# A limit of six transfers in flight on SyncE's queue, in a cosine attention with a token-mixing MLP behind it

## The chip, the cores and the metric

The kernel runs on one core of one Trainium2 chip. A core has five engines with their own instruction streams: TensorE (PE in the profile, its weight loads PEld), VectorE (DVE), ScalarE (ACT), GpSimd (POOL) and SyncE (SP), and 16 DMA engines that move data between memory and the on-chip buffers. SP here does nothing but issue transfers. The metric is device microseconds of one execution. Before the change the median of six runs is 131.78 us (129.74 to 132.66).

## The reference

Eight batches, eight heads, 576 positions, 64 features per head, all in float32. The first part is a linear attention whose features are weighted by the cosine and sine of the position, the second a mixing of tokens:

```python
theta = pi/2 * arange(576)/576
q_p = concat(relu(q)*cos(theta), relu(q)*sin(theta))    # per head, 128 features
k_p = concat(relu(k)*cos(theta), relu(k)*sin(theta))
kv  = einsum('bhsf,bhsd->bhfd', k_p, v);  z = sum(k_p, over s)
x   = (q_p @ kv) / (q_p . z + 1e-6)                     # heads joined: (8, 576, 512)
wq, wk = x @ w_q, x @ w_k                               # 512 -> 64
mixed  = (wq @ wk.T / 8) @ x
out    = relu(mixed) @ w_out                            # (8, 576, 512)
```

## The kernel before

The 64 heads are taken two at a time: a tile holds two heads, one on each half of the 128 partitions, with 9 rows of 64 features in each partition, which is 128 x 576 float32 or 288 KB. Two such tiles make one step H (0 to 15), with halves s = 0 and 1. So q, k and v come in as 96 loads of 288 KB each; the weights come in three more, the output leaves in 42 stores of 128 or 256 KB.

For each step the loads `LD` (line 203) fill the float32 tiles `raw` (a ring of `N_RAW` = 4 steps for each of k, q and v; the profile names them kf, qf, vf). `RK` (relu of k) and `MK` (times cosine and sine) make `kp`, `CV` casts v to `vb`, `DQ` makes relu of q twice side by side in `qd`. `QK` on TensorE forms k'v and transposes q; `EK` and `EQ` bring both out of PSUM, `NM` makes numerator and denominator, `RC` and `XN` divide, which gives `xs`. After the four pairs of a batch: `XT`, `WQK`, `TK`, `KX`, `MX`, `WO` are the products of the second part, `EX`, `EW`, `EWK`, `EKX`, `EMX`, `EO` their way out of PSUM, and `ST` (line 422) stores from `osb`, a ring of `N_OSB` = 6.

The order of all this is written out by hand in `ORDER` (line 37): words such as `LD.k.14.0@Y` name an operation, its step and half, and the engine (Y SyncE, A ScalarE, V VectorE, G GpSimd, T TensorE with a PSUM bank). Each engine executes its words strictly in that order. The framework adds the semaphores: an instruction waits for what it reads and for the users of the buffer that it overwrites. The load of k for step 14, for example, overwrites the tile of step 10 and waits for `RK.10.0@A`; everything behind it on SyncE waits with it. The 129 transfers of SyncE are the 96 loads, the three loads of weights (`LW`, lines 213 to 216) and 30 of the stores, in the order of the words; 12 stores are ScalarE's. Completion of transfers is told by eight semaphores that are taken in turn by all transfers in the order of the program; a transfer whose semaphore was used before waits for the landing of that earlier transfer.

Of the kernel before, what the change touches and what calls it, by code (L numbers as in the profile page):

```python
# [24 lines left out]
N_RAW, N_RK, N_KP, N_QD, N_VB, N_QPT, N_KV = 4, 2, 3, 3, 3, 4, 4  # L25
N_XS, N_XT, N_WQK, N_WKJ, N_KX, N_MIX, N_OSB = 3, 2, 2, 2, 2, 2, 6
# [3 lines left out]
SPLIT = (0, 1, 2, 3, 4, 5, 6, 7, 8, 9, 10, 11, 12, 13, 14, 15)  # L30
UNITS = (((0, 1), (2, 3)), ((0,), (1, 2), (3, 4)))
UNITS7 = ((0,), (1, 2), (3,), (4,))
N_FIRST, N_WARM = 9, 14


# [74 lines left out]
def kernel(  # L110
# [14 lines left out]
    DH = moe_w_q.shape[1]  # L125
    P = 128
# [12 lines left out]
    def ring(name, shape, dtype, n):  # L139
        return [consts.tile(shape, dtype, name=f"{name}{i}") for i in range(n)]  # L140

    raw = {t: ring(f"{t}f", [P, 2, HC], FP32, N_RAW) for t in "kqv"}
# [14 lines left out]
    osb = ring("osb", [P, 2, DM], FP32, N_OSB)  # L157
    w_f = consts.tile([P, NDM, 2 * DH], FP32, name="w_f")
    wo_f = consts.tile([P, NDM, DM], FP32, name="wo_f")
# [21 lines left out]
    A, V, G, T, Y = nc.scalar, nc.vector, nc.gpsimd, nc.tensor, nc.sync  # L181
# [18 lines left out]
    def part(H, s):  # L200
        return (s, s + 1) if H in SPLIT else (0, 2)

    def LD(eng, pb, t, H, s):
        lo, hi = part(H, s)
        b, h = divmod(H, 2)
        step = 1 if LD_PAIR else hi - lo
        for i in range(lo, hi, step):
            eng.dma_start(raw[t][H % N_RAW][:, i:i + step, :],  # L208
                          srcs[t][b][:, 2 * h + i:2 * h + i + step, :])

    def LW(eng, pb, w):
        if w == "qk":
            eng.dma_start(w_f[:, :, 0:DH], moe_w_q.rearrange("(c p) j -> p c j", p=P))
            eng.dma_start(w_f[:, :, DH:2 * DH], moe_w_k.rearrange("(c p) j -> p c j", p=P))
        else:
            eng.dma_start(wo_f, moe_w_out.rearrange("(c p) n -> p c n", p=P))

    def CW(eng, pb, w, s=0):
        if w == "qk":
# [172 lines left out]
    def EMX(eng, pb, b, j):  # L392
# [9 lines left out]
        else:  # L402
            eng.tensor_scalar(dst, src, scale_moe, 0.0, op0=ALU.mult, op1=ALU.max)

    units = [(b, u, ts) for b in range(B)
             for u, ts in enumerate(UNITS7 if b == B - 1 else UNITS[b % 2])]
    unit_of = {(b, t): (n, ts) for n, (b, u, ts) in enumerate(units) for t in ts}
# [14 lines left out]
    def ST(eng, pb, b, u, hi):  # L422
        ts = (UNITS7 if b == B - 1 else UNITS[b % 2])[u]
        n, _ = unit_of[b, ts[0]]
        bl, c = divmod(2 * (ts[0] + 4 * (b % 2)) + hi, C9)
        row = ((b // 2) * 2 + bl) * S + c
        dst = dataclasses.replace(
            out, offset=out.offset + row * DM,
            ap=[[C9 * DM, 64], [2 * DM, len(ts)], [1, DM]])
        eng.dma_start(dst, osb[n % N_OSB][64 * hi:64 * hi + 64, 0:len(ts), :])  # L430

    ops = dict(LD=LD, LW=LW, CW=CW, RK=RK, MK=MK, CV=CV, DQ=DQ, QK=QK, EK=EK, EQ=EQ,
               NM=NM, RC=RC, XN=XN, XT=XT, EX=EX, WQK=WQK, EW=EW, DW=DW, TK=TK,
               EWK=EWK, KX=KX, EKX=EKX, MX=MX, EMX=EMX, WO=WO, EO=EO, ST=ST)
    engines = dict(T=T, V=V, A=A, G=G, Y=Y)

# [72 lines left out]
```

## Time and profile before

| | |
|---|---|
| median of six runs | 131.78 us (129.74 to 132.66) |
| profiled execution: time, span | 132.43 us, 130.6 us |
| busy: DVE, PE, ACT, POOL | 105.7, 103.7, 77.4, 70.3 us |
| mean granted TensorE clock | 0.927 |
| transfers: bytes, mean rate | 39.40 MB, 302 GB/s |
| chain that ended last | PE 30%, DVE 29%, DMA 13%, issue 7%, POOL 6%, SP 5% |
| SP's longest wait for an engine | 8.3 us, for ScalarE's relu of k (L193) |

Busy times are those of the engines' data paths; SP has none, since issuing is not counted. "From issue to landing" is the time from the start of the issuing instruction to the last update of the transfer's semaphore. The chain is followed back from the last instruction, at each step to what released it. In views by time the span starts at 0.

### The profile page before, as it was taken

What the parts mean: (1) busy time and instruction counts of PE and PEld (TensorE: products, weight loads), DVE (VectorE), ACT (ScalarE), POOL (GpSimd) and SP (SyncE); (2) the same over time, 40 slices, a digit from 0 to 9 for tenths busy, and PEclk for the clock granted to TensorE, in tenths of its full rate; (3) what the DMA queues carried; (4) which work ended last, traced back from release to release, by engine and by line L of the source; (5) the groups of instructions that cost most, each with busy time, mean ns of one, the idle gap of its engine ahead of it and who ended that gap; (6) DMA issues with size and microseconds to landing.
All of it is one profiled execution on the core that took longest, in us unless ns stands there. A gap on an engine that the chain in (4) does not pass through costs nothing.

```text
span 130.6 us, 5197 instructions
## 1 busy us (share of the span) xinstructions
PE 103.7 (79%) x2198; PEld 68.6 (53%) x2198; DVE 105.7 (81%) x227; ACT 77.4 (59%) x124; POOL 70.3 (54%) x81
## 2 busy tenths in 40 slices
PE   5925694848789979769999939779999979999900
PEld 2315584738577546556667627355676754543400
DVE  3466999897999999999999865899999987774600
ACT  7125443983596688974948828637986644246110
POOL 7009826098969999992095341589949540020000
PEclk9995559595999999999999999999999999999997
DMA  4999999999999999990079999999998897369793
GB/s 149 288 381 406 398 385 376 348 389 385 395 380 390 391 378 393 385 348 29 5 188 374 255 317 385 355 365 328 355 336 331 163 359 219 83 203 282 179 287 100
DMA packets 20711, 39.40 MB, mean 302 GB/s; under 512 B 3280, under 2 KB 3280, under 8 KB 20688
## 3 DMA queue, kind: packets, MB, share of 16 engines
q1 hardware_dynamic: 19152, 36.32, 80.9%
q10 hardware_dynamic: 1536, 2.75, 6.6%
q8 instruction: 17, 0.28, 0.8%
q14 instruction: 6, 0.05, 0.1%
HBM read 29.62 MB, written 9.44 MB: 299 GB/s over the span
## 4 chain that ended last, share of the span: by engine, by line
PE 30%; DVE 29%; DMA 13%; issue 7%; POOL 6%; SPq 5%; ACT 4%; ACTq 2%; POOLq 0%
PE banks L413 13%; DVE kp L232 9%; DMA kf<-in_k_dram 9%; DVE xs L309 8%; DVE qpt L279 6%; DMA qf<-in_q_dram 5%; PE banks L260 4%; PE banks L269 4%; POOL qd L195 3%; SPq L208 3%; DVE rec L305 3%; PE banks L326 2%; SPq L430 2%; PE banks L292 2%; DVE kvs L187 2%
## 5 line engine op out<-in xcount | busy, mean ns | idle before, releaser
L195 POOL TENSOR_SCALAR qd<-qf 128x1152 bf16<-128x1152 f32 x32 | 38.5, 1213 | 13.8 <-DMA qf<-in_q_dram 13.1
L413 PE MATMUL banks<-wo_sb,mix 128*128 128x512 bf16 x144 | 36.0, 380 | 0.0
L232 DVE TENSOR_TENSOR kp<-rk,cossin 128x1152 bf16<-128x1152 bf16 x32 | 28.9, 923 | 1.8 <-POOL rk L195 1.5
L309 DVE TENSOR_TENSOR xs<-banks,rec 128x640 bf16<-128x640 f32 x32 | 25.4, 807 | 0.3
L279 DVE TENSOR_TENSOR qpt<-banks,cst 128x1152 bf16<-128x1152 bf16 x32 | 23.8, 744 | 2.3 <-PE banks L269 2.0
L185 ACT COPY osb<-banks 128x512 f32<-128x512 f32 x31 | 18.0, 589 | 12.8 <-PE banks L413 9.0
L401 ACT ACTIVATE mix<-banks 128x640 bf16<-128x640 f32 (+1 forms) x27 | 17.4, 657 | 10.2 <-PE banks L388 10.0
L260 PE MATMUL banks<-vb,kp 64*128 64x65 bf16 x576 | 16.7, 202 | 6.2 <-ACT vb L185 2.0
L413 PEld LDWEIGHTS <-mix 128*128 128x128 bf16 x144 | 12.1, 98 | 12.5 <-issue 1.6
L260 PEld LDWEIGHTS <-kp 64*128 64x128 bf16 x576 | 13.6, 101 | 9.6 <-issue 3.7
L269 PE MATMUL banks<-ident,qd 64*128 64x64 bf16 x576 | 16.4, 203 | 2.4 <-POOL qd L195 2.4
L292 PE MATMUL banks<-kvs,qpt 128*128 128x65 bf16 x320 | 15.6, 200 | 3.1 <-DVE kvs L187 2.2
L292 PEld LDWEIGHTS <-qpt 128*128 128x128 bf16 x320 | 13.4, 101 | 6.9 <-DVE qpt L279 2.3
L195 POOL TENSOR_SCALAR rk<-kf 128x576 bf16<-128x576 f32 x14 | 12.4, 893 | 6.4 <-DMA kf<-in_k_dram 6.0
L193 ACT ACTIVATE rk<-kf 128x576 bf16<-128x576 f32 x15 | 10.1, 684 | 9.2 <-DMA kf<-in_k_dram 9.2
L189 POOL TENSOR_SCALAR vb<-vf 128x576 bf16<-128x576 f32 x17 | 12.5, 738 | 5.2 <-DMA vf<-in_v_dram 4.1
L269 PEld LDWEIGHTS <-qd 64*128 64x128 bf16 x576 | 13.1, 103 | 2.5 <-POOL qd L195 2.5
L185 ACT COPY xT<-banks 128x1280 bf16<-128x1280 bf16 x10 | 12.3, 1227 | 3.6 <-PE banks L326 3.6
L185 ACT CAST vb<-vf 128x576 bf16<-128x576 f32 x14 | 9.4, 674 | 6.2 <-DMA vf<-in_v_dram 5.9
L326 PE MATMUL banks<-ident,xs 64*128 64x64 bf16 x320 | 7.8, 196 | 5.4 <-DVE xs L309 5.3
L326 PEld LDWEIGHTS <-xs 64*128 64x128 bf16 x320 | 6.4, 99 | 8.5 <-DVE xs L309 5.1
L189 POOL TENSOR_SCALAR wq<-wqk 64x576 bf16<-64x576 bf16 x4 | 2.8, 708 | 14.9 <-DVE wqk L187 7.8
(46 smaller groups left out, 115.0 us busy)
## 6 DMA issues: line engine op xcount, KB each, us to landing
kf<-in_k_dram SPq DMA_DIRECT2D x32, 288.0 KB, 5.9
vf<-in_v_dram SPq DMA_DIRECT2D x32, 288.0 KB, 6.0
qf<-in_q_dram SPq DMA_DIRECT2D x32, 288.0 KB, 5.9
out_dram<-osb SPq DMA_DIRECT2D x21, 256.0 KB, 4.7
out_dram<-osb ACTq DMA_DIRECT2D x9, 256.0 KB, 4.2
out_dram<-osb SPq DMA_DIRECT2D x9, 128.0 KB, 3.5
wo_f<-in_moe_w_out_dram SPq DMA_DIRECT2D x1, 1024.0 KB, 7.9
out_dram<-osb ACTq DMA_DIRECT2D x3, 128.0 KB, 4.1
```

The lines of the kernel that those rows point to most:

```text
L185: A.copy(dst, src)
L189: eng.tensor_scalar(dst, src, 1.0, 1.0, op0=ALU.mult, op1=ALU.mult)
L195: eng.tensor_scalar(dst, src, FMAX, 0.0, op0=ALU.min, op1=ALU.max)
L232: eng.tensor_mul(kp[H % N_KP][:, lo:hi], rk[H % N_RK][:, lo:hi].unsqueeze(3).to_broadcast([P, n, C9, 2, D]), cossin.unsqueeze(1).to_broadc ...
L260: T.matmul(kvp[:, hh, :], kp[H % N_KP][p0:p0 + 64, i, c, :, :], vb[H % N_VB][p0:p0 + 64, i, c, 0:D + 1], start=(c == 0), stop=(c == C9 - 1))
L269: T.transpose(qt[:, hh, c * D:(c + 1) * D], src, ident[p0:p0 + 64, p0:p0 + 64])
L279: eng.tensor_mul(qpt[g % N_QPT][:, :, 1:SLOTS, :], qk_views(at["QK", g])[0].rearrange("f h (c d) -> f h c d", c=C9), cst.unsqueeze(1).to_b ...
L292: T.matmul(nv[:, hh, u, :], qpt[g % N_QPT][:, hh, 2 * u:2 * u + 2, :], kvs[g % N_KV][:, hh, :], start=(u == 0), stop=(u == SC - 1 and not ...
L309: eng.tensor_tensor(xs[b % N_XS][:, :, 2 * pr:2 * pr + 2, :].rearrange("p u h d -> p h u d"), num_view(at["NM", g])[:, :, :, 0:D], rec[g % ...
L326: T.transpose(xv[:, r, i, u, :], xs[b % N_XS][p0:p0 + 64, u, 2 * hp:2 * hp + 2, :], ident[p0:p0 + 64, p0:p0 + 64])
L401: A.activation(dst, src, AF.Relu, scale=scale_moe)
L413: T.matmul(o, mix[b // 2 % N_MIX][:, dmc, base:base + P], wo_sb[:, dmc, :], start=(dmc == 0), stop=(dmc == NDM - 1))
```

## The change

A function `dma` takes the place of the direct calls. It issues as before, keeps a list of the transfers that were issued on SyncE, and from the seventh on makes each of them depend on the one six places ahead in that list, so that it is issued only after that one has landed. Transfers on ScalarE's queue go through the same function and are neither listed nor held.

```diff
+N_FLIGHT = 6
...
+    flight = []
+
+    def dma(eng, dst, src):
+        ins = eng.dma_start(dst, src).ins
+        if eng is Y:
+            if len(flight) >= N_FLIGHT:
+                tc.add_manual_dep(ins, flight[-N_FLIGHT].name, mybir.DependencyInfo(
+                    mybir.DependencyClass.Sync, mybir.DependencyReason.DATA),
+                    reason="limit on transfers in flight")
+            flight.append(ins)
+
     def LD(eng, pb, t, H, s):
...
-            eng.dma_start(raw[t][H % N_RAW][:, i:i + step, :],
+            dma(eng, raw[t][H % N_RAW][:, i:i + step, :],
                           srcs[t][b][:, 2 * h + i:2 * h + i + step, :])
...
-            eng.dma_start(w_f[:, :, 0:DH], moe_w_q.rearrange("(c p) j -> p c j", p=P))
-            eng.dma_start(w_f[:, :, DH:2 * DH], moe_w_k.rearrange("(c p) j -> p c j", p=P))
+            dma(eng, w_f[:, :, 0:DH], moe_w_q.rearrange("(c p) j -> p c j", p=P))
+            dma(eng, w_f[:, :, DH:2 * DH], moe_w_k.rearrange("(c p) j -> p c j", p=P))
         else:
-            eng.dma_start(wo_f, moe_w_out.rearrange("(c p) n -> p c n", p=P))
+            dma(eng, wo_f, moe_w_out.rearrange("(c p) n -> p c n", p=P))
...
-        eng.dma_start(dst, osb[n % N_OSB][64 * hi:64 * hi + 64, 0:len(ts), :])
+        dma(eng, dst, osb[n % N_OSB][64 * hi:64 * hi + 64, 0:len(ts), :])
```

## The prediction

> **What bounds the kernel now.** I read first which stretches are full of transfers, then what SyncE (SP) waits for, then whether a transfer's 6 us is work or queue, and last who uses the data. From the page, the transfer load in 40 slices of 3.27 us and the median time from issue to landing:
>
> ```profile
> DMA  4999999999999999990079999999998897369793
> ...
> kf<-in_k_dram SPq DMA_DIRECT2D x32, 288.0 KB, 5.9
> vf<-in_v_dram SPq DMA_DIRECT2D x32, 288.0 KB, 6.0
> qf<-in_q_dram SPq DMA_DIRECT2D x32, 288.0 KB, 5.9
> ```
>
> The engines that move data are full from 3 to 59 us, empty from 59 to 64, and nearly full again to about 100. SP's own waits up to 54.8 us:
>
> ```profile
> SPq L208 <- DMA qf<-in_q_dram: 7.0, 17, 0.8
> SPq L208 <- DMA vf<-in_v_dram: 6.6, 16, 0.7
> SPq L208 <- DMA kf<-in_k_dram: 6.5, 16, 0.9
> SPq L208 <- DMA wo_f<-in_moe_w_out_dram: 2.3, 1, 2.3
> ```
>
> The reader is to see that SP already waits for landings, about fifty times and 0.4 us each. The trace gives the distance: eight completion semaphores are used in turn, and an issue waits for the landing of the transfer eight earlier (the load issued at 52.44 follows, by 0.06 us, one that landed at 52.38). The kernel before is therefore limited to eight; the change makes that six. SP's timeline shows the pace:
>
> ```profile
> 50.89 0.33 SPq L208 DMA_DIRECT2D qf<-in_q_dram  x1
> 51.66 0.33 SPq L208 DMA_DIRECT2D vf<-in_v_dram  x1
> 52.44 0.33 SPq L208 DMA_DIRECT2D qf<-in_q_dram  x1
> 53.19 0.33 SPq L208 DMA_DIRECT2D kf<-in_k_dram  x1
> ```
>
> An issue takes 0.33 us, one follows the other after 0.75 us, and 288 KB (294,912 bytes) in 0.75 us is 393 GB/s. Eight times 0.75 is 6.0 us, which is the time to landing: most of the 5.9 us may be queue. Two views say that it is. The first load after the pause, issued at 64.44 into empty queues (transfers issued from 64.4 to 64.8 us):
>
> ```profile
> kf<-in_k_dram SPq DMA_DIRECT2D x1, 288.0 KB, 2.8
> ```
>
> The very first load, at 0.74, took 2.7. And the drain: SP issues nothing between 55.2 and 64.4 us, since the load of k for pair 14 waits for ScalarE (8.3 us in SP's waits), so what is in flight falls from eight to none. By stretch (length; busy time of PE, PEld, DVE, ACT, POOL; granted clock; transfer share; GB/s):
>
> ```profile
> 40.00:55.20 15.20, 13.57 (x291) 8.41 (x289) 14.80 (x32) 12.05 (x21) 14.56 (x16) 1.00 1.05 388
> ...
> 55.20:56.20 1.00, 0.91 (x8) 0.73 (x8) 1.00 (x2) 0.62 (x2) 0.92 (x2) 1.00 1.03 385
> 56.20:57.20 1.00, 1.00 (x46) 0.92 (x46) 1.00 (x2) 0.73 (x2) 0.92 (x2) 1.00 1.03 371
> 57.20:58.20 1.00, 0.34 (x19) 0.25 (x12) 0.99 (x3) 0.97 (x3) 1.00 (x2) 1.00 1.01 378
> ```
>
> The rate stays at 371 to 385 GB/s while six, five, four remain, and the last eight landings (55.37 to 60.46) keep a spacing of 0.73 us down to the last one. The transfer engines don't need eight to be full.
>
> Where is data late? Up to 24 us nearly every relu or cast starts 0.02 to 0.2 us after its load's landing; from 24 to 59 DVE is 97% busy (14.80 of 15.20 us above) and loads have 0.1 to 5 us to spare. From 64.4 to 87 loads are just in time again, and the chain that ended last runs through two of them:
>
> ```profile
> 68.43 4.37 DMA kf<-in_k_dram
> ...
> 74.00 7.00 DMA kf<-in_k_dram
> ```
>
> **The change, part by part.** No byte, no transfer and no instruction of another engine is added or moved. Added is one wait on each SP issue but the first six (123 of 129 issues; ScalarE's 12 stores are neither counted nor held).
>
> *Instructions.* Where all transfers are SP's, the new wait covers the old one: the transfer eight earlier was already waited for by the issue two before. So one wait takes the place of one, and its reaction is 0.02 us as now. Where ScalarE's stores lie between (from 73 us), an issue may need a second wait; such separate waits stand in the trace with 0.02 us and some 0.05 us around them. With 12 such stores: 0 to 12 x 0.07 = 0.8 us, and of these only those from 73 to 87, where SP's issues are on the chain, can count (two stores, 0.1 us). I take 0.1 us.
>
> *Start (to 6.6 us).* The seventh issue stands at 3.54 and the transfer six ahead landed at 3.44: no hold. The eighth goes from 4.01 to 4.21, the ninth from 4.75 to 6.57 (landing of the third at 6.55). The ninth landed at 11.09; issued by 6.9 it has 4.2 us left, against 2.8 for a whole lone load. Cost 0; the queue of transfers four to eight covers it.
>
> *Full stretch (6.6 to 55.2 us).* Each issue moves two spacings later: 2 x 0.75 = 1.5 us. Its landing was 5.9 after the issue, so 4.4 remain, and a lone load needs 2.7 to 2.8. The cover is 1.6 us, some two transfers always queued. So landings stay and cost is 0. Behind each held issue on SP stand only later issues, held by the same pace; who waits for them (relu and cast on ACT, POOL, DVE) waits for landings. Without that cover each 0.1 us of spacing would cost 1.7 us on the 17 loads up to 24 us. Behind the 1 MB load of w_out (landed 36.01) two more issues wait (from 32.57 and 33.36 to about 36.03 and 36.8); they landed at 41.22 and 41.96, so about 5 us remain. Cost 0.
>
> *Pause (55.2 to 64.4).* Ended by ScalarE's relu of k at 63.73, which hangs on DVE and PE work. Unchanged.
>
> *Late loads (64.4 to 82).* Here the time goes, so I compared each issue with the landing six before it on SP. Of the issues from 64.44 to 81.69 the tightest stand 0.00 to 0.06 us after it (74.85, 76.43, 77.62, 78.28, 81.69), the rest 0.2 to 7.6 us. On this stretch a six-back wait on SP's list and the present eight-back wait over both queues are nearly the same, since two of ScalarE's stores lie between. Cost 0, with nothing to spare: a hold here would go straight to the end.
>
> *82 to 97.* Holds of 0.1 to 1.5 us; 3.3 to 4.6 us remain to each landing. Here SP issues almost without pause (18 issues from 82.23 to 96.07, 0.77 us each), yet transfers are 101% busy at 350 GB/s, so SP loses run-ahead and not landings. At 96.8 it stands still for ScalarE's copy until 100.39 anyway. Cost 0.
>
> *Stores at the end (from 100).* The transfer six ahead had landed 1.2 to 11 us before. Cost 0.
>
> The sum: 0.1 us on the profiled execution's 132.43 (span 130.6). That run lies above the median of the six, 131.78; on the median it gives 131.9.
>
> The Trainium skill speaks against the change in one place. The page "DMA: Bandwidth & Descriptors", section "Rules for kernel authors", advises to issue a DMA early and wait for it late, so that its fixed cost overlaps. If landings moved with the issues, that rule would make the just-in-time loads 1.5 us later and the time 133.4; the drain above shows landings that don't depend on it.
>
> **Rivals.**
> 1. *Slower: the window no longer covers engines that fall behind.* Code fetches ride on the same 16 engines: the page has 17 instruction packets at 0.8% of 16 x 130.6 us, about 1 us each, on one engine. Two of the seven before 54 us show as a spacing of 1.46 us in place of 0.75 (SP's issues at 17.18 and 18.64, 36.77 and 38.28); the others don't, since different engines fall behind and the queue lets the rest run ahead. Six leave 1.6 us for that, eight leave 3.1. If the spread passes 1.6 us, up to five more such pauses of 0.7 us come before 54 us, 3.5 in all, and two from 82 to 97, 1.4; less some 0.6 of slack in use that is 4.3: 136.1. Three pauses are 1.5 and stay within 2%; it ends slower by 2% (2.6 us) from five on. Against it: two queued transfers are more than one packet's delay.
> 2. *Slower by much: the 5.6 us after an issue is travel, not queue.* Then six give 6 transfers in 5.95 us, 0.99 each: +0.24 x 17 = 4 us by 24 us, up to 15 by the pause, 136 to 147. The lone 2.7 to 2.8 us speak against it.
> 3. *Faster: less in flight moves faster.* From 4 to 7 us the rate is 301 GB/s, beside 388 later, while SP issues without pause; held issues might let it rise: 3 x (1 - 301/388) = 0.7 us. A spacing of 0.71, as in the last landings of the drain, in place of 0.75 would give 17 x 0.04 = 0.7 by 24 us, and up to 1.9 more by 54 if compute were not the limit there. Together -1.4 to -3.3; 130.4 to 128.5. Against it: the rate in the drain at four to six is not higher than at eight.
> 4. *The change does not do what it says*: its waits are covered by the present ones everywhere, 131.8. Then SP's issues would keep their eight-back pace.
>
> **How the numbers follow.** Forecast as worked out, 131.9 (0.54), own range 130.5 to 133.3 from the scatter of the six runs (129.74 to 132.66); rival 4: 0.04; rival 1: 0.20, of which 0.16 is over 2% (2% is about what a measurement of this kernel can tell from no change); rival 2: 0.06; rival 3: 0.16, half of it over 2%. So faster 0.08, same 0.54 + 0.04 + 0.04 + 0.08 = 0.70, slower 0.16 + 0.06 = 0.22. The range leaves out rival 2, the top of rival 1 and the low half of rival 3: 129.8 to 135.6.
>
> **What would show it.** Time to landing of the loads falls from 5.9 to about 4.5 us; SP's waits grow little in the full stretch (a landing per 0.75 us as before) and its issues there follow the landing six before; the stretch 40 to 55 keeps 388 GB/s; the pause before 64.4 keeps its end. I am wrong if the rate there falls below 370, if more pauses of 1.4 us stand between SP's issues, or if the loads issued from 64 to 82 us are held by the new wait.

## The result, and the profile after

| | before | after |
|---|---|---|
| median, us | 131.66 (74 executions, 129.74 to 134.36) | 133.41 (32 executions, 131.0 to 136.83) |
| profiled execution: time, span | 132.43, 130.6 us | 132.77, 131.0 us |
| time ratio | 1 | 1.0075 [1.0045, 1.0105] |
| busy: DVE, PE, ACT, POOL | 105.7, 103.7, 77.4, 70.3 us | 106.2, 105.7, 77.6, 69.0 us |

The change costs 0.75%, some 1.0 us, by the ratio and 1.3%, 1.75 us, by the medians; both are within 2% of no change. The medians take in every execution, while the ratio, here and in the experiments, takes only the executions within 1.5% of the fastest of their kernel, which are 14 of after, two of mv8 and two of mv6. The executions of after scatter more widely.

The small number hides a large movement. The page's transfer load and rate in 40 slices of 3.27 us, the instruction packets, and the median time from issue to landing, after:

```profile
DMA  4999999999999999999988999999999798479693
GB/s 141 319 395 370 377 382 339 307 355 314 312 343 334 309 372 338 349 315 348 327 228 253 258 355 334 399 344 336 346 284 294 192 361 247 111 191 288 177 283 103
...
q8 instruction: 17, 0.28, 0.9%
...
kf<-in_k_dram SPq DMA_DIRECT2D x32, 288.0 KB, 5.0
vf<-in_v_dram SPq DMA_DIRECT2D x32, 288.0 KB, 4.8
qf<-in_q_dram SPq DMA_DIRECT2D x32, 288.0 KB, 5.2
```

The rate before:

```profile
GB/s 149 288 381 406 398 385 376 348 389 385 395 380 390 391 378 393 385 348 29 5 188 374 255 317 385 355 365 328 355 336 331 163 359 219 83 203 282 179 287 100
```

The reader is to see two things. From the seventh slice (20 us) to the pause the rate is 307 to 372 GB/s where the kernel before had 348 to 395; and the two empty slices around 60 us, the pause of before, are gone: they now carry 348 and 327. The loads land 4.8 to 5.2 us after their issue instead of 5.9 to 6.0.

Busy time by stretch (length; busy time of PE, PEld, DVE, ACT, POOL; granted clock; transfer share; GB/s), before:

```profile
10.00:55.00 45.00, 35.22 (x908) 26.76 (x909) 41.49 (x88) 30.75 (x47) 35.34 (x35) 0.82 1.06 386
55.00:64.00 9.00, 7.55 (x183) 5.60 (x181) 8.86 (x20) 6.58 (x12) 4.61 (x5) 1.00 0.44 161
```

The same stretches after, and the one from 40 to 55 us for which the prediction had named a rate:

```profile
10.00:55.00 45.00, 36.14 (x912) 26.72 (x913) 41.47 (x89) 30.77 (x47) 30.60 (x32) 0.81 0.99 343
55.00:64.00 9.00, 8.04 (x218) 5.96 (x217) 8.86 (x20) 7.47 (x14) 7.48 (x8) 1.00 0.98 344
...
40.00:55.00 15.00, 13.98 (x293) 8.50 (x291) 14.33 (x32) 11.86 (x21) 12.40 (x15) 1.00 0.98 339
```

The rate from 10 to 55 us falls from 386 to 343 GB/s. From 10 to 64 us the bytes are nevertheless almost the same: 386 x 45 + 161 x 9 = 18.8 MB before, 343 x 45 + 344 x 9 = 18.5 MB after. The lost rate is paid out of the pause. DVE, the busiest engine here, is busy for 41.5 of the 45 us in both: compute didn't slow down in this execution. The loads became late by 6.1 us (the last one ahead of the pause landed at 60.46 before, at 66.58 after), and that was lead that nobody used.

What is left of the pause stands in SP's waits from 55 us on. Before (55 to 65 us):

```profile
SPq L208 <- ACT rk L193: 8.3, 1, 8.3
```

and after (55 to 64 us):

```profile
SPq L207 <- ACT rk L194: 1.3, 1, 1.3
```

ScalarE's relu that ends this wait started at 63.73 us before and at 62.86 after: its end didn't move outward, and SP arrives later.

Where the rate goes is seen in SP's timeline of after (start, length) around 28 us:

```profile
26.17 0.33 SPq L207 DMA_DIRECT2D vf<-in_v_dram  x1
26.86 0.33 SPq L207 DMA_DIRECT2D qf<-in_q_dram  x1
29.91 0.33 SPq L207 DMA_DIRECT2D kf<-in_k_dram  x1
30.67 0.33 SPq L207 DMA_DIRECT2D vf<-in_v_dram  x1
```

and in the stretches across this gap (columns as above):

```profile
26.90:29.90 3.00, 1.81 (x23) 1.10 (x23) 3.00 (x4) 1.34 (x3) 2.08 (x2) 0.50 0.99 361
29.90:30.50 0.60, 0.60 (x29) 0.60 (x24) 0.60 (x2) 0.26 (x1) 0.00 (x0) 0.50 1.05 407
30.50:31.25 0.75, 0.75 (x36) 0.75 (x32) 0.50 (x2) 0.75 (x1) 0.00 (x0) 0.50 0.82 206
31.25:34.00 2.75, 2.71 (x70) 2.24 (x65) 1.97 (x5) 0.64 (x3) 2.41 (x4) 0.78 0.92 283
```

For 3.06 us (26.84 to 29.90) no transfer landed, and after the issue at 26.86 SP issued nothing, yet 361 GB/s kept moving. The reading: most of the 16 engines ran ahead into the queued transfers while at least one was behind, and a transfer has landed only when its last engine is done. (On that last point the Trainium skill, "DMA: Bandwidth & Descriptors", section "Why a DMA increments its semaphore by 16 and not by 1", says that a transfer's engines finish independently and the semaphore counts them.) Then the five transfers behind landed at the usual 0.73 us, but from 30.5 us on the engines that had run ahead ran short, since SP had been held by the late landing: 206 GB/s, and 283 up to 34 us. That is the loss.

A packet of code fetching (16 KB, about 1 us on one engine) stands at 27.39 us. Between landings, after has eight delays of 0.30 us and more from 10 to 66.6 us, with 8.1 us beyond the normal spacing of 0.75 us, or 2.7 us for the 1 MB of w_out (2.3 in this one, 1.4 for the load of w_out, 0.3 to 1.3 in the others). Seven of the eight, 7.5 of the 8.1 us, end 2.5 to 3.5 us after the start of a code packet; nine such packets start between 14 and 64 us. By the same count before has three delays with 2.2 us, though it fetches as often. The difference, 5.9 us, is about the 6.1 us by which the loads were late.

The chain that ended last, by engine, has more transfers in it, 21% against 13%; its largest pieces on transfers after the pause, start and length:

```profile
66.75 5.38 DMA out_dram<-osb
72.14 5.95 DMA vf<-in_v_dram
```

The load issued at 72.14 stood at 72.23 before. From 65.4 to 74 us SP's issues lie within 0.35 us of those of before; the next one comes 1.8 us later (76.63 for 74.85), and by 80 us the loads are level again.

### The profile page after: what moved, and what is told of

Read it like the earlier page. It is cut to its first block, busy times and chain, and to the rows that moved or that the text cites. A ratio compares the mean times of both kernels' runs of the same rounds, so it can differ in the third digit from the quotient of the medians.

```text
span 131.0 us, 5200 instructions
## 1 busy us (share of the span) xinstructions
PE 105.7 (81%) x2198; PEld 69.1 (53%) x2198; DVE 106.2 (81%) x227; ACT 77.6 (59%) x124; POOL 69.0 (53%) x81
## 4 chain that ended last, share of the span: by engine, by line
PE 33%; DVE 27%; DMA 21%; POOL 5%; ACT 3%; issue 3%; SPq 2%; ACTq 2%; POOLq 0%
PE banks L425 13%; DVE kp L244 11%; DMA kf<-in_k_dram 8%; DVE xs L321 5%; DVE qpt L291 5%; DMA vf<-in_v_dram 5%; PE banks L272 4%; DMA out_dram<-osb 4%; DMA qf<-in_q_dram 4%; PE banks L304 3%; PE banks L281 3%; PE banks L383 3%; POOL qd L196 3%; PE banks L355 2%; SPq L207 2%
## 5 line engine op out<-in xcount | busy, mean ns | idle before, releaser
L196 POOL TENSOR_SCALAR qd<-qf 128x1152 bf16<-128x1152 f32 x32 | 39.1, 1233 | 13.6 <-DMA qf<-in_q_dram 12.8
L425 PE MATMUL banks<-wo_sb,mix 128*128 128x512 bf16 x144 | 36.8, 387 | 0.0
L186 ACT COPY osb<-banks 128x512 f32<-128x512 f32 x31 | 18.0, 589 | 15.5 <-PE banks L425 10.9
L304 PE MATMUL banks<-kvs,qpt 128*128 128x65 bf16 x320 | 16.3, 202 | 3.6 <-DVE kvs L188 2.2
L190 POOL TENSOR_SCALAR vb<-vf 128x576 bf16<-128x576 f32 x17 | 13.3, 782 | 9.7 <-DMA vf<-in_v_dram 6.2
L281 PE MATMUL banks<-ident,qd 64*128 64x64 bf16 x576 | 15.9, 200 | 2.3 <-POOL qd L196 2.3
L281 PEld LDWEIGHTS <-qd 64*128 64x128 bf16 x576 | 12.7, 101 | 2.4 <-POOL qd L196 2.4
L196 POOL TENSOR_SCALAR rk<-kf 128x576 bf16<-128x576 f32 x14 | 9.6, 694 | 6.8 <-DMA kf<-in_k_dram 6.4
L355 PE MATMUL banks<-xT,wqk_sb 128*128 128x288 bf16 x64 | 10.1, 306 | 0.3 <-DVE xT L188 0.2
```

The lines of the kernel that those rows point to most:

```text
L186: A.copy(dst, src)
L190: eng.tensor_scalar(dst, src, 1.0, 1.0, op0=ALU.mult, op1=ALU.mult)
L196: eng.tensor_scalar(dst, src, FMAX, 0.0, op0=ALU.min, op1=ALU.max)
L281: T.transpose(qt[:, hh, c * D:(c + 1) * D], src, ident[p0:p0 + 64, p0:p0 + 64])
L304: T.matmul(nv[:, hh, u, :], qpt[g % N_QPT][:, hh, 2 * u:2 * u + 2, :], kvs[g % N_KV][:, hh, :], start=(u == 0), stop=(u == SC - 1 and not ...
L425: T.matmul(o, mix[b // 2 % N_MIX][:, dmc, base:base + P], wo_sb[:, dmc, :], start=(dmc == 0), stop=(dmc == NDM - 1))
```

## The experiments

Two theories. **Spread**: the time to landing is queue (as the prediction had it), but engines fall behind one another by more than two queued transfers cover, and then the others run dry; the pause pays for the lateness. **Travel** (the prediction's second rival): six in flight simply can't carry the rate. Besides, whether the 0.75% comes from the lost rate before the pause, from the loads after it, or from SP's added waits alone.

### Four kernels of transfers alone

From the kernel with the limit; all compute and the three loads of weights are left out, what is stored is zeros, and the stores are all SP's. The two with `_pe` put 1800 small matmuls beside the transfers, with no other tie to them.

```diff
+    for t in osb:
+        V.memset(t, 0.0)
...
+    V.memset(warm, 1.0)                       # _pe only
+    for _ in range(1800):                     # _pe only
+        T.matmul(bank1(7, 0, 400, FP32), warm[:, 0:P], warm[:, 0:100], start=True, stop=True)
+    work = [w for w in work if w.startswith("LD.")] + [
+        w.split("@")[0] + "@Y" for w in work if w.startswith("ST.")]
-N_FLIGHT = 6
+N_FLIGHT = 8                                  # stream8, stream8_pe
```

Eight, no compute:

> Transfers alone: the 96 loads in the order of the kernel, then its 42 stores (of zeros), all on SyncE, limit eight; no TensorE, ScalarE or GpSimd work and VectorE only clears the output tiles, so the output is not computed. Both theories: loads at 0.74 to 0.76 us each, about 390 GB/s, 96 loads landed by 75 us.

Six, no compute:

> The same transfers alone with the limit of six. Spread theory (engines fall behind through code fetches, which this kernel hardly has): the same rate as with eight, within 2 %. Depth theory (six in flight are slower by themselves, since the queues run thin): 330 to 350 GB/s, as in the changed kernel, loads landed 8 us or more later than with eight.

Eight, with matmuls:

> Transfers alone as before, limit eight, beside 1800 matmuls of TensorE on a constant tile that read no load: they add only TensorE's code, which is fetched by the same transfer engines in packets of 16 KB. Spread theory: about 380 GB/s, a few of the fetches visible as a late landing.

Six, with matmuls:

> The same with limit six. Spread theory: each fetch leaves a pause of 0.7 us or more between landings, 340 to 360 GB/s, 5 to 8 us later than eight by the last load. Depth theory: the same as the transfers alone with six. If both are at the rate of eight, what slows the changed kernel is the traffic of the engines on the buffers, which this kernel lacks.

| | stream8 | stream6 | stream8_pe | stream6_pe |
|---|---|---|---|---|
| span, us (one execution each) | 111.2 | 113.4 | 114.7 | 123.4 |
| last of the 96 loads landed, us | 75.9 | 76.1 | 78.0 | 86.0 |
| issue to landing of loads, us | 6.0 | 4.5 | 6.0 | 4.6 to 5.3 |
| delays of over 0.2 us between landings of loads, from 10 us on | 0 | 1 | 2 | 12 |
| their sum, us | 0 | 0.3 | 2.6 | 11.5 |

The stretch from 10 to 55 us, without matmuls (columns: DVE, POOL, granted clock, transfer share, GB/s), eight:

```profile
10.00:55.00 45.00, 0.00 (x0) 0.00 (x0) 1.00 1.05 393
```

six:

```profile
10.00:55.00 45.00, 0.00 (x0) 0.00 (x0) 1.00 1.05 391
```

With matmuls (PE and PEld ahead of these columns), eight:

```profile
10.00:55.00 45.00, 44.53 (x968) 44.09 (x967) 0.00 (x0) 0.00 (x0) 1.00 1.05 390
```

six:

```profile
10.00:55.00 45.00, 44.91 (x975) 44.80 (x974) 0.00 (x0) 0.00 (x0) 1.00 1.00 353
```

Travel falls: six alone carry 391 GB/s, and the time to landing shrinks to 4.5 us, exactly six spacings. What spread expects is there: with the matmuls six lose 10% of the rate and eight lose 1%. The page of stream6_pe shows the code fetches of the matmuls, which the two kernels without PE don't have:

```profile
q8 instruction: 14, 0.23, 0.7%
```

and SP's timeline one of the delays, at 2.13 us between issues in place of 0.75:

```profile
30.32 0.77 SPq L207 DMA_DIRECT2D qf<-in_q_dram  x1
32.45 0.33 SPq L207 DMA_DIRECT2D vf<-in_v_dram  x1
```

Six of the twelve delays follow the start of a code packet by 2.5 to 3.0 us: five of them are of this size (1.4 to 1.5 us beyond the spacing), one is 1.0 us. They make 8.1 of the 11.5 us. The others don't line up with a packet, and these kernels can't separate PE's fetches from PE's other work for them. With eight in flight 11 fetches fall among the loads, with six 12; eight leave two delays, of 1.3 us each and again 2.5 to 2.6 us behind a packet's start, and the other nine fetches show none.

### Other limits

```diff
-N_FLIGHT = 6
+N_FLIGHT = 8        # fl8, and once more as fl8b
+N_FLIGHT = 4        # fl4
```

> The limit at eight instead of six, nothing else. On SyncE's list a wait for the eighth transfer back is nearly the wait that the kernel before already has. Spread theory (six leave too little lead for engines of the transfer hardware that fell behind through a code fetch): the pauses between landings go, the rate from 10 to 55 us returns from about 345 to 385 GB/s, ratio 1.000 (0.997 to 1.003). If the added dependency itself cost the time (more waits on SyncE), the ratio stays at 1.006 to 1.010.

> The limit at four. Lead of an issue over its landing: 4 x 0.74 = 3.0 us, a lone load takes 2.7 to 2.8, so nothing is left for an engine that falls behind. Spread theory: every code fetch shows in full and small delays too, rate from 10 to 55 us 270 to 310 GB/s, the loads of the first 60 us come 15 us or more late, the pause of SyncE at 55 to 64 us is used up and can't hide that: ratio 1.05 to 1.12. If six cost only something fixed (a wait per issue), four costs the same as six: 1.008.

With eight the limit binds no earlier than the semaphores on SP's own queue, so what is tested is the wait itself. fl8: 132.8 us (11 executions) beside 131.56, ratio 1.0142 [1.0074, 1.021]. That would be a cost of the waits alone; so the same kernel was timed once more, on another chip:

> The limit of eight once more (the kernel of the run with eight, 11 executions, 1.014). It differs from the kernel before in seven of SyncE's issues alone, which wait for a second transfer. If that ratio was scatter of the loads behind the pause: 0.995 to 1.005. If those seven waits cost: again 1.008 to 1.02, and then a part of the loss with six is the second waits behind ScalarE's stores and not the number in flight.

fl8b: 131.4 (12 executions) beside 132.44, ratio 1.0028 [0.9969, 1.0087]. Two series of one kernel, each beside the kernel before on its own chip, give intervals that hardly meet. So 11 or 12 executions leave about 1% open here, whatever the interval says, and a cost of the second waits isn't shown. What the profiles do show is that the rate nearly stays, 380 GB/s from 10 to 55 us (fl8b):

```profile
10.00:55.00 45.00, 36.02 (x904) 27.16 (x908) 41.49 (x88) 30.72 (x47) 33.68 (x35) 0.78 1.05 380
```

Four: 151.64 us (147.92 to 156.11, 5 executions), 15% over the 131.56 beside it, more than the 5 to 12% expected. In the profiled execution, the slowest of the five, the time to landing is 4.2 us, and

```profile
10.00:55.00 45.00, 30.67 (x720) 23.88 (x720) 33.96 (x73) 23.15 (x34) 23.14 (x24) 0.70 0.87 273
```

The rate is 273 GB/s and DVE is busy 34 of 45 us: the loads are now what compute waits for. The load of k for pair 14, which the pause used to hold to 64.4 us, is issued at 77.0 with no wait for ScalarE. Between six and four the pause is used up, and behind it everything is time.

### The limit on one side of the pause

```diff
-            if len(flight) >= N_FLIGHT:
+            if N_FLIGHT <= len(flight) <= 70:     # first6: up to the pause
+            if len(flight) >= 71:                 # last6: behind it
```

> The limit of six only for the first 71 transfers of SyncE (up to the load of k for pair-step 11, half 1), none from the pause on. Cover theory: the loads up to 62 us come 5 to 7 us later, but the load that ends the pause, and what follows it, is issued at 63.5 to 64.5 us as in the kernel before: ratio 0.997 to 1.003. If the late loads of the first 60 us are what the changed kernel loses: 1.006 to 1.013, as with the whole change.

> The other half: no limit for the first 71 transfers of SyncE, six from the load of k for step 14 on. Cover theory: the first 64 us are those of the kernel before, and the loss of the change sits in the loads from 64 to 100 us, which have no slack and where fewer in flight cover less of each code fetch: ratio 1.006 to 1.013. If the loss comes from the first stretch: 0.997 to 1.003.

| | first6 | last6 |
|---|---|---|
| median, us (beside 132.44) | 133.25 (12 executions) | 131.89 (13 executions) |
| ratio | 1.0089 [1.0009, 1.017] | 1.0073 [1.0002, 1.0144] |
| load of k, pair 14, issued, us | 63.86 | 65.81 |

The stretches of first6 repeat the picture of the changed kernel:

```profile
10.00:55.00 45.00, 33.94 (x905) 25.72 (x910) 41.81 (x89) 31.30 (x48) 30.98 (x32) 0.85 0.99 348
55.00:64.00 9.00, 8.03 (x206) 6.02 (x208) 8.86 (x20) 6.92 (x13) 7.03 (x8) 1.00 0.96 325
```

while last6 keeps 381 and 172 GB/s there. So the rate is lost by the limit up to the pause and not by the limit behind it; and in first6's profile SP still waited 2.9 us for ScalarE's relu, so the lost rate was again covered there. The 0.75% isn't placed. By the ratios each half shows as much as the whole, with intervals that nearly reach 1, and for first6 that is the number of the rival (1.006 to 1.013) and not of the cover; by the medians first6 is 0.6% above the kernel beside it and last6 0.4% below. After fl8 and fl8b neither can be believed to half a per cent.

### Taking the cover away: the load that makes the pause

If the pause pays for the lost rate, a kernel without the pause should show the price. The load of k for pair 14 is put ten transfers later on SP, so that it no longer holds the others while it waits for ScalarE's relu; mv8 does that to the kernel before, mv6 to the one with the limit.

```diff
-... EW.3@A LD.k.14.0@Y MK.10.1@V WO.1.4@T6 ...
+... EW.3@A MK.10.1@V WO.1.4@T6 ...
...
-LD.v.11.0@Y XT.8@T6 ...
+LD.v.11.0@Y LD.k.14.0@Y XT.8@T6 ...
```

> The kernel before with one word of the order moved: SyncE's load of k for step 14, half 0, behind the load of v for step 11, half 0, so that the ten transfers behind it no longer wait for ScalarE's relu of k for step 10. If the pause of SyncE from 55.4 to 64.4 us costs the kernel before the late loads that follow it, the loads for step 11 land before 66 us instead of 70 to 78, and the time falls by 2 to 4 us: ratio 0.97 to 0.985. If PE and DVE work bounds that stretch anyway: 0.995 to 1.0.

> The kernel with the limit of six, with the same word moved. Cover theory: in the changed kernel the loads up to 60 us land some 6 us later, and SyncE's pause, which is 8 us long before and 1.3 us long after, pays for it; without the pause in the order there is little left to win for six: at most 1.3 us, ratio to the kernel before 0.995 to 1.005, and 1.5 to 3 % above the same order with eight. If the loss of the limit came elsewhere (late loads from 64 us on, stores), six would gain by the move as eight does and stay 0.7 % above it.

mv8: 129.98 us (127.17 to 130.88, 11 executions) beside 131.56, ratio 0.977 [0.9666, 0.9874], 1.2% between the medians: faster than both kernels, with its slowest execution below the median beside it. mv6: 136.04 (131.83 to 137.5, 5 executions), ratio 1.0151 [0.9956, 1.0346]; no execution of mv6 is as fast as the slowest of mv8. With the pause gone, six against eight is 1.0151 / 0.977, 3.9%, and 4.7% between the medians, where it was 0.75% and 1.3%, and where 1.5 to 3% had been expected; with five executions of mv6 the size is rough, the direction isn't.

Where mv8 gains: the stretch that carried 161 GB/s now carries 352, and the loads behind it are early. From 72 to 80 us, mv8:

```profile
72.00:80.00 8.00, 6.66 (x175) 4.53 (x174) 7.93 (x15) 5.36 (x11) 7.76 (x9) 1.00 1.02 357
```

and the kernel before:

```profile
72.00:80.00 8.00, 5.68 (x163) 4.18 (x162) 5.78 (x12) 4.47 (x9) 2.78 (x3) 1.00 0.96 306
```

POOL's wait for k between 64 and 92 us falls from 6.0 to 0.9 us, the load of v for pair 12 lands at 71.3 instead of 79.65, DVE is busy 7.93 of 8 us instead of 5.78, and the chain that ended last is compute (transfers 4% instead of 13%):

```profile
DVE 44%; PE 30%; issue 7%; POOL 5%; DMA 4%; SPq 2%; ACT 2%; ACTq 2%; POOLq 0%
```

mv6's loss isn't all rate. From 50 us on its loads land 4 to 7 us later than mv8's, from 78 us on over 9; the load of k is issued at 72.45 without any wait for ScalarE; and then ScalarE stands still in front of one of its own stores, from 74.64 to 81.73 us. ScalarE's waits from 64 to 92 us, mv6:

```profile
ACT vb L186 <- DMA kf<-in_k_dram: 7.8, 1, 7.8
```

(The row's 7.8 us take in the issue of the store, 0.72 us, which comes between.) The store's completion semaphore had last been used by a load of k that SP issued at 74.17 and that landed at 81.71. mv8 has the same tie; that load's landing isn't recorded there, but the one ahead of it landed at 71.31, and the store was issued at 73.41. So a late load on one queue stops an engine that has no use for it. How mv6's loss divides between this wait and late data wasn't separated.

One more move on top of mv8: the last load of v ahead of a store that waits for ScalarE.

```diff
-... EKX.5@A ST.4.1.1@Y XN.28@V ... LD.v.15.1@Y CV.14.1@G ...
+... EKX.5@A LD.v.15.1@Y ST.4.1.1@Y XN.28@V ... CV.14.1@G ...
```

> No limit, SyncE's load of k for step 14 moved behind the load of v for step 11 as before, and the load of v for step 15, half 1, put ahead of the store of batch 4 (unit 1, upper half) that SyncE waits 4.8 us for. If transfers that stand behind a waiting one are what the kernel loses, the second move takes the 2.7 us in which GpSimd waits for that load off the chain: 1 to 2 us below the first move alone, ratio 0.96 to 0.975. If TensorE bounds that stretch, as its share of the chain there suggests: 0.975 to 0.985, as the first move alone.

129.61 us (127.87 to 131.32, 6 executions) beside 132.44, ratio 0.9882 [0.9736, 1.0029]. Its interval overlaps that of mv8: the second move isn't resolved. In its profile POOL's wait for that load is gone, and the end is where mv8 had it (span 127.8 against 127.9): the chain there passes through a store and PE instead.

## Why the prediction was right or wrong

The time lies in the range and the sign of "within 2%" was right, at 133.4 by the median of all executions and 0.75% by the ratio, where 131.9 had been put. But the likeliest case was right for a reason that didn't hold, which is luck: loads became 6 us later that were to stay where they were, and a pause that the sum had at nothing paid for it. The 133.4 that the prediction gives for just-in-time loads 1.5 us later equals the measured median by chance too: those loads weren't later throughout (see *Late loads*).

*Instructions* (0.1 us). The engines' other instructions are the same, and no profile shows a larger cost. fl8 and fl8b, which test the waits alone, bound it only to about 1%.

*Start* (0). Held; the seventh transfer landed at 8.86 us instead of 9.59, but over all the kernels it lies between 8.68 and 9.59, the 8.68 without a limit. So rival 3's 0.7 us isn't there: that is scatter.

**The step that failed is the full stretch** (landings stay, 388 GB/s, 0). The rate fell to 339, below the 370 that I had named as refuting it, and the landings came up to 6.1 us later. The reasoning "time to landing is queue" was right: stream6 has 4.5 us and 391 GB/s. Wrong was the step from the drain of before (371 to 385 GB/s with six, five, four left) to "two queued transfers, 1.6 us, are cover enough". The drain lasted 5 us and no landing in it was late; the cover is needed when an engine falls behind. And rival 1, which had this mechanism, priced one fetch at 0.7 us from the two delays that eight in flight let through in the kernel before; stream8_pe shows 1.3 us each, stream6_pe up to 1.5, and after one of 2.3.

*Pause* ("unchanged", ended at 63.73 by ScalarE). Its end was right within a microsecond: 62.86. Its size wasn't: SP's wait shrank from 8.3 to 1.3 us. I used the pause only as evidence on the queue, and not as what it is in the sum: 8 us by which every load ahead of it may be late at no cost. Rival 1 lists "some 0.6 of slack in use" at the point where this belongs. Its sum up to the pause was 3.5 of delays less 0.6 of slack; measured are 5.9 more of delays against 7.0 of pause used, so this part becomes nothing. Its other 1.4, for two delays from 82 to 97 us, has no pause behind it. That is why rival 1's mechanism came with about the forecast's time.

*Late loads* (0, "nothing to spare"). SP's issues from 65.4 to 74 us lie within 0.35 us of before, so the new waits don't hold them there. From 76.6 to 82.2 us each issue follows the landing six before by 0.0 to 0.1 us; the first stands 1.8 us later than before, because that landing is 1.8 us later (76.61 for 74.85), the next three 0.5 to 0.9 later, and from 80 us on they are no later than before. "Nothing to spare" was right; but before, the issues from 74.85 to 78.28 us follow the same landings as closely, so a new hold isn't shown. The engines' waits for transfers from 64 to 92 us add up to 15.5 us instead of 12.7 in the profiled executions; two profiles of the kernel with eight lie further apart (7.3 and 15.9).

*82 to 97, and stores at the end* (0). In the profile of after the issues there stand up to 3.0 us later, where holds of up to 1.5 us had been put, the landings from 94 to 103 us are 0.8 to 1.2 us later, and the last stores are issued 0.35 us later, about the difference of the two spans. It is one execution, and no run tests these parts alone.

*What would show it*: time to landing 4.8 to 5.2 us and not 4.5 (the delays stretch it; 4.5 comes only where there are none); the issues of the full stretch do follow the landing six back, mostly by 0.02 to 0.06 us, which refutes rival 4; the rate and the count of delays went against me.

**Open:** where the 0.75% comes from. Neither half of the limit could be shown to cost something, or nothing. Explanations that fit but were only argued: the later landings from 94 us on; or six leave 1.3 us (after) to 2.9 us (first6) of SP's wait at the pause, eight leave 8.3, and in some executions the delays exceed that; the wider scatter of after would agree.

## What to carry to other kernels

The number of transfers in flight that was needed here isn't bandwidth times the time of a lone transfer alone (393 GB/s x 2.8 us, 1.1 MB or four transfers); it has to cover too how far one of the engines falls behind the others. Six of 288 KB (1.8 MB) carry the full rate alone and lose 10% beside 1800 matmuls and their code fetches, eight (2.4 MB) lose 1%. A rate that is lost upstream of a pause costs little (here 0.75 to 1.3%) until the pause is used up (4.7% without it), so before pricing a slower stretch look for the next place where its queue waits for an engine, and compare the two; the same wait, read the other way, is the place to gain: moving the one load that made it gave 1.2% between the medians (129.98 us beside 131.56), and 2.3% by the ratio, which rests on two executions.

## What the runs showed of the hardware that was not expected

- One 16 KB code fetch, about 1 us by its own record, can delay the landings behind it by 1.4 to 1.5 us (five times in stream6_pe). The fetches take 0.7% of the transfer engines' time there, and the short queue loses 10% of its rate beside the matmuls; 8.1 of the 11.5 us of delays stand behind a fetch, the rest isn't explained.
- While no transfer landed for 3.06 us, 361 GB/s kept moving: a gap between landings isn't a gap in transfer, it becomes one only when the next issue hangs on the late landing.
- A completion semaphore used in turn by two queues made ScalarE wait 7.1 us (74.64 to 81.73) for a load of SyncE's that it had no use for.
- Two series of 11 and 12 executions of the same kernel, on two chips, gave 1.0142 and 1.0028.
